# Conversion of weights under up 1: another order of the blocks, and higher prices in the planner's books

## The chip, the core and the metric

The kernel runs on one core of a Trainium2 chip. The metric is the device time of one execution in microseconds (us). The engines are TensorE (PE, with its weight loads as PEld), VectorE (DVE), ScalarE (ACT), GpSimd (POOL) and SyncE (SP), which issues the transfers.

## What is computed

A random-feature attention is followed by two feed-forward networks, all in float32 (2304 tokens, width 512):

```python
q_p, k_p = (phi(q_s), phi(k_s))
num = np.einsum('bhsm,bhmd->bhsd', q_p, kv)          # attention
h = x @ w_in                                         # "up 1"
x = (h * (1.0 / (1.0 + np.exp(-h)))) @ w_out         # "down 1"
g = x @ w_gate;  val = x @ w_val                     # "up 2"
return (silu(g) * val) @ w_out2                      # "down 2"
```

The weights come in as float64 and have to be turned into float32 on the chip before they can be used.

## The kernel before

**Stages.** Attention comes first (up to about 118 us), then up 1, down 1, up 2 and down 2. Each of the four products of matrices is done by Strassen's scheme with seven products per block (`PROD`, `ORDER`), and each float32 operand is split into a high and a low part, so that a product is three matmuls (high-high, high-low, low-high). Up 1 is a sequence `seq1` of 24 steps: a step is one block of 256 of the hidden features (there are eight, 0 to 7) for one of three groups of 768 tokens. The first nine steps take blocks 0, 1, 2 for each group of tokens in turn, the next three block 3, the next three block 4, and the last nine blocks 5, 6, 7. A step is seven products of six matmuls each. Between the products of a step, ScalarE copies a PSUM bank (L1120: `copy`), VectorE adds (L1177), ScalarE applies the activation (L1144: `post`), and SyncE stores the result to memory as `g_d` (L1129: `put`). The operands made of x are split beside it by ScalarE and VectorE (L586, L597, L619: `x_prep`).

**Conversion.** `conv_job` makes a list of operations for one block of float64 weights, in two halves h. Two loads of 512 KB (`load`, L328) go into raw buffers (`f_raw`, two at first). ScalarE turns the high words (`first`, L349) into a conversion buffer (`f_c`, three at first). VectorE shifts it (`shift`, L356) and puts in bits of the low words (`low`, L363). GpSimd makes four sums and differences of Strassen's scheme (`sums`, L382) into the one sum buffer (`f_sum`). What comes then depends on the weights. Blocks for up 1 ("in i") are split into high and low (L411 to L429) into an operand space (`f_w`, room for three blocks, taken first by blocks 0, 1 and 2). Blocks for down 1 ("out i", `down_job`) and the gate and value block for up 2 (`up_job_dram`) are stored to memory in three transfers (`store`, L446) and loaded later (L1282), and then split (L1286, L1290). The sum buffer and the conversion buffers are free when the splitting, or the store, is done. More buffers of both kinds are given (`more`) when the splitting of x has been handed out. Blocks 0 to 2 of both weights are converted during attention (`feed`, which goes by steps, not by times). The other twelve jobs run under up 1: in 3, out 3, in 4, out 4, ..., in 7, out 7, gate, val, in this order, joined by `weave`, which puts the first half of a job's list between the last operations of the job before. The first two loads of in 3 are issued at the end of attention.

**The planner.** All instructions are issued from one Python program; each engine works off its own queue in the order in which the program emitted. The program keeps books: `clk` has a time for each engine and for the transfers, `T` the time at which each result is there, and an `Op` has a price. `flush` is called ahead of every product. It emits operations whose turn has come by the books: first those in `urgent` (copies, additions, activations, stores of g), then of the streams the one that could start first, with a handicap of 0.1 us for each place in the list of streams (loads of g, weights of down, splitting for down, splitting of x, conversion). The conversion's stream looks one operation further on ScalarE (`ACT=2`). `need` emits at once what a product cannot do without. The prices come from `cost(kind, n)`, a constant and a rate for each engine (`fixed`); a transfer takes its bytes at 350e3 bytes per us of the books' transfer clock and lands 3.0 us later. The loads of g for down 1 (`zload`) wait until the conversion's stream is empty (a `guard`).

Of the kernel before, what the change touches and what calls it, by code (L numbers as in the profile page):

```python
# [42 lines left out]
def kernel(  # L43
# [19 lines left out]
    S = 576  # L63
# [16 lines left out]
    FP = (w_in.shape[0], w_gate.shape[0])  # L80
# [20 lines left out]
    def cut(t, o, n):  # L101
        return t[:, o : o + n]
# [14 lines left out]
    class Free:  # L117
# [17 lines left out]
        def give(self, x, t=None):  # L135
# [3 lines left out]
                return  # L139
            self.q.append((x, clk["PE"] if t is None else t))  # L140

    clk = {e: 0.0 for e in ("PE", "ACT", "DVE", "POOL", "SP", "dma", "slot")}
    T = {}
    fixed = {"ACT": (0.21, 0.00081), "DVE": (0.15, 0.00106), "POOL": (0.25, 0.0021), "COPY": (0.1, 0.0006)}

    def cost(kind, n):
        a, b = fixed[kind]
        return a + b * n

    class Op:  # L150
# [22 lines left out]
        def emit(self):  # L173
            t = max(clk[self.eng], self.ready())
            clk["slot"] = 0.0
            clk["end"] = t + self.cost
            self.fn()
            if self.eng == "SP":
                clk["SP"] = t + 0.3
                clk["dma"] = max(t, clk["dma"]) + self.cost  # L180
                end = clk["dma"] + 3.0
            else:
                clk[self.eng] = end = t + self.cost
            for k in self.outs:
                T[k] = end
            if self.then is not None:
                self.then(end)

    def dma_cost(nbytes):
        return nbytes / 350e3  # L190

    urgent = []
    maker = {}
# [118 lines left out]
    f_c = Free("c", [cut(fa, C_AT + i * 512, 512) for i in range(3)])  # L312
# [5 lines left out]
    w_slots = [x for x, _ in f_w.q]  # L318
    W = {}

    def conv_job(kind, i, dram=None, side=False):
        b = {}
        key = lambda *k: (kind, i, *k)

        def load(h):
            def go():
                b["r", h] = r = f_raw.take()
                nc.sync.dma_start(out=r.bitcast(U32), in_=wsrc[kind][i, h])  # L328

            def then(end):  # L330

                if kind == "out2":
                    T[key("r", h)] = end + 6.0

            return Op("SP", dma_cost(P * 4096), go, outs=[key("r", h)], slots=(f_raw, 1), then=then)

        def word(h, w):
            return b["r", h].bitcast(U32).rearrange("p (c w) -> p c w", w=2)[:, :, w]

        def first(h):  # L340
            def go():
                b["c", h] = c = f_c.take()

                nc.scalar.activation(c, word(h, 1).bitcast(F32), AF.Prelu, scale=2.0**-112, alpha=-(2.0**32))  # L349

            return Op("ACT", cost("ACT", 512), go, ins=[key("r", h)], outs=[key("c", h)], slots=(f_c, 1))

        def shift(h):
            def go():
                c = b["c", h].bitcast(U32)
                nc.vector.tensor_scalar(c, c, 3, None, op0=ALU.logical_shift_left)  # L356

            return Op("DVE", cost("COPY", 512), go, ins=[key("c", h)], outs=[key("s", h)])

        def low(h):  # L360
            def go():
                c = b["c", h].bitcast(U32)
                nc.vector.scalar_tensor_tensor(  # L363
                    c, word(h, 0), 29, c, op0=ALU.logical_shift_right, op1=ALU.bitwise_or
                )
                f_raw.give(b["r", h], clk["end"])

            return Op("DVE", cost("DVE", 512), go, ins=[key("s", h)], outs=[key("f", h)])

        def blk(n):  # L370
            if n in ("A21", "A22"):
                return cut(b["c", 0], 0 if n == "A21" else 256, 256)
            if n in ("A11", "A12"):
                return cut(b["c", 1], 0 if n == "A11" else 256, 256)
            return cut(b["S"], 256 * (int(n[1]) - 1), 256)

        def sums(n, l, r, ins):
            def go():
                if n == 1:
                    b["S"] = f_sum.take()  # L380
                f = nc.gpsimd.tensor_add if n == 1 else nc.gpsimd.tensor_sub
                f(blk(f"S{n}"), blk(l), blk(r))  # L382

            return Op(
                "POOL", cost("POOL", 256), go, ins=[key(*k) for k in ins], outs=[key("S", n)],
                slots=(f_sum, 1) if n == 1 else None,
            )

# [50 lines left out]
        def store(a, z, src, ins):  # L439

            b["stores"] = 3

            def go():
                o = dram(a, z)
                t = src()
                nc.sync.dma_start(out=o, in_=t.rearrange("p (o c) -> p o c", c=256) if len(o.shape) == 3 else t)  # L446
                b["stores"] -= 1
                if not b["stores"]:
                    done(clk["end"] + 2.0)

            return Op("SP", dma_cost(P * (z - a) * 1024), go, ins=[key(*x) for x in ins], outs=[key("d", a)])

        half = [load(0), load(1), first(0), first(1), shift(0), low(0), shift(1), low(1)]
        if dram is not None:
            return [
# [36 lines left out]
    def weave(*jobs):  # L492

        ops = [*jobs[0][:8]]
        for n, j in enumerate(jobs):
            new = deque(jobs[n + 1][:8] if n + 1 < len(jobs) else ())
            for _ in range(min(2, len(new))):
                ops.append(new.popleft())
            for i, o in enumerate(j[8:]):
                ops.append(o)  # L500
                if i % 2 and new:
                    ops.append(new.popleft())
            ops += new
        return ops

    def down_job(m, i):
        k = DNK[m]
        return conv_job(
            k, i, dram=lambda a, z: wd_d[k][a:z, :, i * 256 : (i + 1) * 256].rearrange("o p c -> p o c")
        )  # L510

    def up_job_dram(k):
        return conv_job(k, 0, dram=lambda a, z: wu_d[k][:, a * 256 : z * 256])
# [464 lines left out]
    for name in ("conv", "x"):  # L978
        while early[name]:
            assert early[name][0].ready() is not None  # L980
            early[name].popleft().emit()
            while urgent:
                urgent.pop(0).emit()
    first_up = conv_job("in", 3)
    for x in first_up[:2]:
        x.emit()
    for f, some in ((f_c, spare_c), (f_sum, [spare_sum])):
        n = len(f.q)
# [4 lines left out]
    for k in T:  # L993
        T[k] = 0.0
    for h, t in enumerate((4.0, 6.0)):
        T["in", 3, "r", h] = t
    for f in (f_raw, f_c, f_sum, f_z, f_w, f_s, f_op):
        f.q = deque((x, 0.0) for x, _ in f.q)

# [510 lines left out]
    def up_order(kinds, n, head, tail):  # L1510
# [4 lines left out]
            pairs[-3:] = [(n - 3, n - 2, n - 1)]  # L1515
        return [(i, k, s) for ps_ in pairs for s in range(NSB) for i in ps_ for k in kinds]

    to_come += [
        lambda: x_prep(0, 1, xr1, False, "DVE", then=lambda t: (x1_done.append(t), x1_then[0]())),
        lambda: x_prep(0, 2, xr2, False, "DVE", before=1, then=xr2_end),  # L1520
    ]

    rest = deque(down_job(0, i) for i in range(3, FP[0]))
    jobs = []
    for i in range(3, FP[0]):
        jobs += [conv_job("in", i) if i > 3 else first_up, rest.popleft()]
    jobs += rest
    jobs += [up_job_dram("gate"), up_job_dram("val")]
    conv1 = [x for x in weave(*jobs) if not any(x is y for y in first_up[:2])]
    opened = []  # L1530
    extra_c, extra_raw = cut(fa, XR_AT, 512), cut(fa, XR_AT + 512, 1024)

# [90 lines left out]
    jobs = [down_job(1, 0)]  # L1623
# [75 lines left out]
```

## Time and profile before

| | us |
|---|---|
| median of three runs | 853.46 |
| lowest and highest | 852.75, 853.49 |
| profiled execution | 853.52 |
| its span | 851.7 |

The profile is of one execution of its own, and its span is the time between the first and the last instruction. Times in its rows count from the start of the span. The rows come from several views: a page with the share of each engine and the costliest groups of instructions, tables by stretch of time, lists of waits, and the order of instructions in a stretch. In an order, the text in brackets at the end of a row is how long the engine stood idle before it, and what ended that.

### The profile page before, as it was taken

The numbers are of one execution on the slowest core, as the hardware profiler recorded it, in microseconds if no ns is written. First come the engines' busy times: TensorE is split into PE (matmuls) and PEld (weight loads), VectorE is DVE, ScalarE is ACT, GpSimd is POOL, SyncE is SP. The second block draws the span as 40 slices with busy tenths as digits, with TensorE's granted clock in tenths as the row PEclk, the third lists the DMA queues.
The fourth block names the chain that finished last, engine by engine and source line by source line (L and its number), as shares of the span: only waits on it lengthen the run. The fifth ranks groups of instructions, "written<-read, shape, count | busy, mean of one in ns | idle before, by whom it ended". The sixth has DMA issues, their size and how long they took to land.

```text
span 851.7 us, 18196 instructions
## 1 busy us (share of the span) xinstructions
PE 823.9 (97%) x6889; PEld 796.4 (93%) x6889; DVE 623.8 (73%) x1016; ACT 552.5 (65%) x1166; POOL 164.8 (19%) x204
## 2 busy tenths in 40 slices
PE   8999999999999879999998998999999999999998
PEld 7888889999899879999998998999999999899998
DVE  4888877576644687796899998584757548979783
ACT  6999878776767854455557874655556557646552
POOL 0477831044440000000000035121213010000000
PEclk9999999999999999999999999999999999999999
DMA  8579866588999865608514657462637168483602
GB/s 284 183 259 299 282 211 226 173 260 282 333 310 364 286 231 165 206 22 243 181 62 141 218 179 208 146 204 100 211 97 238 53 212 283 169 272 94 220 3 75
DMA packets 110120, 170.09 MB, mean 200 GB/s; under 512 B 9424, under 2 KB 94032, under 8 KB 110032
## 3 DMA queue, kind: packets, MB, share of 16 engines
q1 hardware_dynamic: 109808, 168.69, 60.9%
q8 instruction: 54, 0.88, 0.4%
q14 instruction: 34, 0.28, 0.1%
q10 hardware_dynamic: 224, 0.23, 0.1%
HBM read 107.02 MB, written 61.87 MB: 198 GB/s over the span
## 4 chain that ended last, share of the span: by engine, by line
PE 76%; DVE 7%; DMA 7%; issue 4%; ACT 3%; POOL 2%; SPq 0%; DVEq 0%; ACTq 0%; POOLq 0%
PE ps L1103 36%; PE ps L1478 29%; PE ps L757 4%; PE ps L801 2%; PE ps L817 2%; DMA wd_out<-fa 2%; PE ps L848 2%; DMA ra<-g_d 2%; POOL fa L382 2%; DVE fa L363 1%; DMA fa<-in_moe_w_val 1%; DVE ra L1341 1%; DMA fa<-in_moe_w_out 1%; DVE ra L429 1%; PE ps L873 1%
## 5 line engine op out<-in xcount | busy, mean ns | idle before, releaser
L382 POOL TENSOR_TENSOR fa<-fa 128x256 f32<-128x256 f32 x124 | 105.6, 866 | 506.4 <-ACT fa L1144 239.3
L1103 PE MATMUL ps<-ra 128*128 128x384 f32 x840 | 148.4, 328 | 6.1 <-ACT ps L1120 4.0
L1103 PE MATMUL ps<-rb,ra 128*128 128x384 f32 x840 | 146.3, 327 | 2.1 <-ACT ps L1120 2.1
L1103 PE MATMUL ps<-rc,ra 128*128 128x384 f32 x840 | 145.8, 326 | 1.5 <-ACT ps L1120 1.5
L1103 PEld LDWEIGHTS ps<-ra 128*128 128x128 f32 x840 | 137.6, 189 | 9.0 <-ACT ps L1120 5.8
L1103 PEld LDWEIGHTS ps<-rb,ra 128*128 128x128 f32 x840 | 137.6, 189 | 3.6 <-ACT ps L1120 3.3
L1103 PEld LDWEIGHTS ps<-rc,ra 128*128 128x128 f32 x840 | 137.8, 189 | 2.5 <-ACT ps L1120 2.4
L1120 ACT ACTIVATE ps<-ps 128x384 f32<-128x384 f32 x180 | 85.4, 477 | 67.7 <-PE ps L1103 63.4
L1177 DVE TENSOR_TENSOR fa<-fa,ps 128x384 f32<-128x384 f32 x120 | 66.2, 551 | 80.5 <-ACT ps L1120 58.0
L1337 ACT ACTIVATE ra<-fa 128x768 fp32r<-128x768 f32 x86 | 71.9, 841 | 60.4 <-PE ps L1478 43.9
L1341 DVE TENSOR_TENSOR ra<-fa,ra 128x768 fp32r<-128x768 f32 x81 | 77.4, 955 | 21.6 <-PE ps L1478 13.4
L1478 PE MATMUL ps<-ra 128*128 128x384 f32 x486 | 84.0, 332 | 6.8 <-DVE ra L1341 5.7
L1478 PE MATMUL ps<-ra,rb 128*128 128x384 f32 x516 | 89.9, 327 | 0.4 <-DVE ra L1341 0.4
L1478 PEld LDWEIGHTS ps<-ra 128*128 128x128 f32 x486 | 80.7, 192 | 9.0 <-DVE ra L1341 7.4
L1478 PE MATMUL ps<-ra,rc 128*128 128x384 f32 x482 | 83.9, 327 | 2.2 <-DVE ra L1341 2.2
L1478 PEld LDWEIGHTS ps<-ra,rb 128*128 128x128 f32 x516 | 84.5, 189 | 1.4 <-DVE ra L1341 1.0
L773 ACT ACTIVATE kq<-ps,nb 128x128 f32<-128x128 f32 x288 | 79.3, 401 | 7.8 <-DVE nb L771 7.5
L1478 PEld LDWEIGHTS ps<-ra,rc 128*128 128x128 f32 x482 | 78.9, 189 | 3.4 <-DVE ra L1341 3.2
L349 ACT ACTIVATE fa<-fa 128x512 f32<-128x512 f32 x65 | 54.0, 833 | 20.2 <-DMA fa<-in_moe_w_in 5.7
L1361 DVE TENSOR_TENSOR fa<-ra,fa 128x768 f32<-128x768 f32 x63 | 60.0, 953 | 4.4 <-DMA ra<-g_d 3.7
L1144 ACT ACTIVATE fa<-fa 128x384 f32<-128x384 f32 x84 | 43.6, 519 | 25.5 <-DVE fa L1177 25.2
L363 DVE SCALAR_TENSOR_TENSOR fa<-fa 128x512 uint32<-128x512 uint32 x65 | 56.0, 862 | 0.7
(112 smaller groups left out, 1104.5 us busy)
## 6 DMA issues: line engine op xcount, KB each, us to landing
g_d<-fa SPq DMA_DIRECT2D x168, 192.0 KB, 4.1
fa<-g_d SPq DMA_DIRECT2D x42, 384.0 KB, 5.0
ra<-g_d SPq DMA_DIRECT2D x42, 384.0 KB, 4.3
fa<-in_moe_w_out SPq DMA_DIRECT2D x28, 512.0 KB, 5.1
fa<-in_moe_w_in SPq DMA_DIRECT2D x16, 512.0 KB, 5.0
wd_out<-fa SPq DMA_DIRECT2D x12, 512.0 KB, 3.2
fa<-in_moe_w_gate SPq DMA_DIRECT2D x12, 512.0 KB, 4.0
fa<-in_moe_w_val SPq DMA_DIRECT2D x12, 512.0 KB, 5.2
```

The lines of the kernel that those rows point to most:

```text
L349: nc.scalar.activation(c, word(h, 1).bitcast(F32), AF.Prelu, scale=2.0**-112, alpha=-(2.0**32))
L363: nc.vector.scalar_tensor_tensor(c, word(h, 0), 29, c, op0=ALU.logical_shift_right, op1=ALU.bitwise_or)
L382: f(blk(f"S{n}"), blk(l), blk(r))
L773: nc.scalar.activation(e[:, g // 2, g % 2, h * M : (h + 1) * M], x[:, g, :], AF.Exp, bias=nb[:, g : g + 1])
L1103: nc.tensor.matmul(woven(ps[b][:, :N]), cut(l, j * P, P), halves(cut(r, j * N, N)), start=start and c == 0, stop=stop and c == 5, skip_gro ...
L1120: nc.scalar.activation(out() if callable(out) else out, src, AF.Copy)
L1144: nc.scalar.activation(b["t"], src, AF.Silu)
L1177: nc.vector.tensor_add(t, t if in_place else p5[n], ps[bank_][:, :N])
L1337: nc.scalar.activation(ops[s, p, k][0], src(), AF.Copy)
L1341: nc.vector.tensor_sub(l, src(), h.bitcast(F32))
L1361: (nc.gpsimd if eng == "POOL" else nc.vector).tensor_sub(z(PLACE[to]), z(PLACE.get(l, l)), z(PLACE.get(r, r)))
L1478: nc.tensor.matmul(woven(ps[BANKS[p] + e][:, :N]), cut(a, e * P, P), halves(b), start=p in FIRST and i == 0 and c == 0, stop=p in LAST and ...
```

## The change

There are four edits. The order of the twelve jobs under up 1 is out 3, out 4, out 5, then in 3, out 6, in 4, out 7, in 5, gate, in 6, val, in 7; accordingly the two loads issued at the end of attention are those of out 3. The books' prices for the conversion go up: `first` 0.85 (it was 0.62), `shift` 0.48 (0.41), `low` 0.9 (0.69), `sums` 1.1 (0.79). All transfers in the books take their bytes at 330e3 per us and land 3.5 us later. And `first` of a job's first half may be handed out only when no other job stands between its two halves (`halved`). The prices and the guard also hold for the conversion under up 2, and the transfers' prices for everything that is planned after attention.

```diff
@@ -139,6 +139,7 @@
+    LAND, RATE = 3.5, 330e3
     clk = {e: 0.0 for e in ("PE", "ACT", "DVE", "POOL", "SP", "dma", "slot")}
@@ -178,7 +179,7 @@
                 clk["dma"] = max(t, clk["dma"]) + self.cost
-                end = clk["dma"] + 3.0
+                end = clk["dma"] + LAND
@@ -187,7 +188,7 @@
     def dma_cost(nbytes):
-        return nbytes / 350e3
+        return nbytes / RATE
@@ -318,6 +319,8 @@
+    halved = []
+
     def conv_job(kind, i, dram=None, side=False):
@@ -340,6 +343,7 @@
             def go():
                 b["c", h] = c = f_c.take()
+                halved[:] = [x for x in halved if x is not b] + ([b] if h == 0 else [])
@@ -348,14 +352,14 @@
-            return Op("ACT", cost("ACT", 512), go, ins=[key("r", h)], outs=[key("c", h)], slots=(f_c, 1))
+            return Op("ACT", 0.85, go, ins=[key("r", h)], outs=[key("c", h)], slots=(f_c, 1), guard=lambda: h == 1 or not halved)
...
-            return Op("DVE", cost("COPY", 512), go, ins=[key("c", h)], outs=[key("s", h)])
+            return Op("DVE", 0.48, go, ins=[key("c", h)], outs=[key("s", h)])
...
-            return Op("DVE", cost("DVE", 512), go, ins=[key("s", h)], outs=[key("f", h)])
+            return Op("DVE", 0.9, go, ins=[key("s", h)], outs=[key("f", h)])
...
-                "POOL", cost("POOL", 256), go, ins=[key(*k) for k in ins], outs=[key("S", n)],
+                "POOL", 1.1, go, ins=[key(*k) for k in ins], outs=[key("S", n)],
@@ -981,8 +985,8 @@
-    first_up = conv_job("in", 3)
-    for x in first_up[:2]:
+    first_down = down_job(0, 3)
+    for x in first_down[:2]:
         x.emit()
@@ -993,7 +997,7 @@
     for h, t in enumerate((4.0, 6.0)):
-        T["in", 3, "r", h] = t
+        T["out", 3, "r", h] = t
@@ -1515,18 +1519,19 @@
+    AHEAD = 3
...
-    rest = deque(down_job(0, i) for i in range(3, FP[0]))
-    jobs = []
+    rest = [first_down, *(down_job(0, i) for i in range(4, FP[0])), up_job_dram("gate"), up_job_dram("val")]
+    jobs = rest[:AHEAD]
     for i in range(3, FP[0]):
-        jobs += [conv_job("in", i) if i > 3 else first_up, rest.popleft()]
-    jobs += rest
-    jobs += [up_job_dram("gate"), up_job_dram("val")]
-    conv1 = [x for x in weave(*jobs) if not any(x is y for y in first_up[:2])]
+        jobs += [conv_job("in", i), *rest[AHEAD + i - 3 : AHEAD + i - 2]]
+    jobs += rest[AHEAD + FP[0] - 3 :]
+    conv1 = [x for x in weave(*jobs) if not any(x is y for y in first_down[:2])]
```

## Rows read from the trace of the kernel before

**Rows 1.** The page's first part: busy us, share of the span, instructions.

```profile
PE 823.9 (97%) x6889; PEld 796.4 (93%) x6889; DVE 623.8 (73%) x1016; ACT 552.5 (65%) x1166; POOL 164.8 (19%) x204
```

**Rows 2.** Busy time by stretch: stretch, length, then engines; granted clock, DMA share, GB/s.

```profile
core 0: us, PE busy (x) PEld busy (x) DVE busy (x) ACT busy (x) POOL busy (x), PEclk, DMA share, GB/s
121.00:132.00 11.00, 10.78 (x68) 10.45 (x67) 9.30 (x20) 8.11 (x18) 3.64 (x4) 1.00 0.96 323
132.00:162.00 30.00, 29.88 (x184) 29.88 (x185) 22.36 (x46) 25.91 (x61) 0.00 (x0) 1.00 0.58 187
162.00:170.00 8.00, 8.00 (x51) 8.00 (x50) 1.93 (x5) 5.00 (x11) 0.00 (x0) 1.00 0.46 162
185.00:200.00 15.00, 13.33 (x81) 12.74 (x80) 9.83 (x18) 10.64 (x23) 7.57 (x9) 1.00 0.92 312
215.00:233.00 18.00, 16.73 (x100) 15.85 (x99) 12.89 (x24) 13.74 (x30) 7.73 (x9) 1.00 0.96 321
233.00:253.00 20.00, 19.20 (x118) 18.80 (x117) 11.17 (x18) 13.24 (x28) 9.42 (x12) 1.00 0.94 327
288.00:297.00 9.00, 6.84 (x39) 5.99 (x38) 6.41 (x8) 6.17 (x11) 0.00 (x0) 1.00 0.65 175
...
470.00:535.00 65.00, 59.91 (x359) 57.74 (x358) 60.12 (x113) 45.16 (x96) 18.49 (x20) 1.00 0.67 207
720.00:742.00 22.00, 20.11 (x119) 18.93 (x118) 20.46 (x27) 15.54 (x23) 0.00 (x0) 1.00 0.56 197
```

**Rows 3.** What TensorE waited for from 118 to 288: total, times, longest.

```profile
PE ps L1103 <- ACT ps L1120: 4.1, 7, 0.9
```

**Rows 4.** ScalarE by line, 170 to 253: count, busy, mean ns, idle before, releasers.

```profile
L349 ACT ACTIVATE fa<-fa 128x512 f32<-128x512 f32 x20 | 17.1, 855 | 12.0 <-DMA fa<-in_moe_w_in 5.7 <-POOL fa L382 4.0 <-DMA fa<-in_moe_w_gate 1.6
```

**Rows 5.** Order of instructions about 194: start, length, engine and line [idle before].

```profile
193.67 0.86 ACT L349 ACTIVATE fa<-fa 128x512 f32<-128x512 f32 x1 [2.32 <-DMA fa<-in_moe_w_in]
...
195.22 0.48 ACT L1120 ACTIVATE ps<-ps 128x384 f32<-128x384 f32 x1
...
195.75 1.24 PE L1103 MATMUL ps<-rb,ra 128*128 128x384 f32 x6 [0.91 <-ACT ps L1120]
```

**Rows 6.** Order of GpSimd's sums under up 1, the first ones and one pair.

```profile
128.53 2.99 POOL L382 TENSOR_TENSOR fa<-fa 128x256 f32<-128x256 f32 x3 [3.23 <-DVE fa L363]
174.04 2.70 POOL L382 TENSOR_TENSOR fa<-fa 128x256 f32<-128x256 f32 x2 [42.52 <-DVE ra L429]
...
182.28 2.92 POOL L382 TENSOR_TENSOR fa<-fa 128x256 f32<-128x256 f32 x4 [3.38 <-DMA wd_out<-fa]
...
197.21 1.42 POOL L382 TENSOR_TENSOR fa<-fa 128x256 f32<-128x256 f32 x2 [3.37 <-DMA wd_out<-fa]
```

**Rows 7.** The page's groups: count, busy, mean ns of one, idle before.

```profile
L382 POOL TENSOR_TENSOR fa<-fa 128x256 f32<-128x256 f32 x124 | 105.6, 866 | 506.4 <-ACT fa L1144 239.3
```

**Rows 8.** The page's transfers: count, KB each, median us from issue to landing.

```profile
fa<-in_moe_w_out SPq DMA_DIRECT2D x28, 512.0 KB, 5.1
...
wd_out<-fa SPq DMA_DIRECT2D x12, 512.0 KB, 3.2
```

**Rows 9.** Order of SyncE's issues about 253.

```profile
253.14 0.32 SPq L446 DMA_DIRECT2D wu_val<-fa  x1
253.55 1.22 SPq L1282 DMA_DIRECT2D ra<-wd_out  x2
```

**Rows 10.** Order of instructions at the hand-over from up 1 to down 1.

```profile
288.80 1.57 ACT L1286 ACTIVATE rb<-rb 128x768 fp32r<-128x768 f32 x2
...
293.33 0.43 PE L1478 MATMUL ps<-ra 128*128 128x384 f32 x1 [1.12 <-ACT ra L1337]
...
306.45 0.96 DVE L1361 TENSOR_TENSOR fa<-ra,fa 128x768 f32<-128x768 f32 x1 [2.37 <-DMA ra<-g_d]
...
308.33 9.89 PE L1478 MATMUL ps<-ra 128*128 128x384 f32 x48 [1.98 <-DVE ra L1341]
```

**Rows 11.** Busy time by stretch, as rows 2, inside down 1's start.

```profile
310.00:312.00 2.00, 2.00 (x8) 2.00 (x8) 1.96 (x3) 1.78 (x3) 0.00 (x0) 0.50 0.41 153
```

More of the change, by code (lines that the diff above doesn't have):

```diff
@@ L1521 @@
     ]
-    rest = deque(down_job(0, i) for i in range(3, FP[0]))
-    jobs = []
+    rest = [first_down, *(down_job(0, i) for i in range(4, FP[0])), up_job_dram("gate"), up_job_dram("val")]
+    jobs = rest[:AHEAD]
     for i in range(3, FP[0]):
-        jobs += [conv_job("in", i) if i > 3 else first_up, rest.popleft()]
-    jobs += rest
-    jobs += [up_job_dram("gate"), up_job_dram("val")]
-    conv1 = [x for x in weave(*jobs) if not any(x is y for y in first_up[:2])]
+        jobs += [conv_job("in", i), *rest[AHEAD + i - 3 : AHEAD + i - 2]]
+    jobs += rest[AHEAD + FP[0] - 3 :]
+    assert len(jobs) == len(rest) + FP[0] - 3
+    conv1 = [x for x in weave(*jobs) if not any(x is y for y in first_down[:2])]
     opened = []
```

## The prediction, made before the changed kernel was run

> **What bounds the kernel now.** I read the page's first part, then a table of busy time by stretch, then who TensorE waited for, and only then the order of work around the worst waits. TensorE is busy 823.9 of 851.7 us [rows 1], so an edit that moves no matmul can win only some of its idle time, and the question is which idle time. The table [rows 2] places it. During up 1's weight conversion TensorE lost 1.67 us (185 to 200), 1.27 us (215 to 233) and 0.80 us (233 to 253), each the stretch minus the PE column. At the hand-over to down 1 it lost 2.16 us (288 to 297). Up 2's start lost 5.09 us and down 2's start 1.89 us. In 132 to 162 it lost only 0.12 us, although ScalarE was busy 25.91 of 30 us: a full ScalarE alone does not stop TensorE.
>
> Every wait of up 1 is for line 1120 [rows 3], ScalarE's PSUM copy between two products. The order shows why [rows 5]: ScalarE stood 2.32 us before a conversion instruction (L349) whose weights had not landed, the copy queued behind it came late, and TensorE lost 0.91 us. Between 170 and 253 ScalarE stood 12.0 us in front of its 20 L349 instructions [rows 4]. So the planner puts conversion into the queue earlier than its data are there.
>
> Why is the conversion so late? GpSimd's sums, of which every block has four, stop at about 131.5 us (128.53 + 2.99) and resume at 174.04 after 42.52 us, released by the block of up 1's weights that got its operand space [rows 6]. That block (in 3) sits on the only sum buffer until block 0's W space is free after step 6. After that a pair (one block for up 1, one for down 1) takes 197.21 - 182.28 = 14.93 us [rows 6]: 74.6 us for five pairs, and the last store of the value weights is issued at 253.14 [rows 9].
>
> **Part 1, the order.** Nothing is computed more or less: twelve blocks stay. Out 3, 4 and 5 now come ahead of in 3, so the sum buffer is turned over three times in the stretch in which it stood still. After 174 the queue before was out 3, in 4, out 4, in 5, out 5, in 6, out 6, in 7, out 7, gate, val. It becomes out 6, in 4, out 7, in 5, gate, in 6, val, in 7: each block of up 1's weights stands where it stood, four pairs are left, and the conversion ends near 174 + 4 x 14.93 = 234 instead of 253. SyncE's loads and stores move with them: out 3's first two loads replace in 3's at the end of attention, of the same size.
>
> *Behind 234*, no L349 is in ScalarE's queue and the 0.80 us of 233 to 253 should go. Term B: **-0.8** (bounds 0 and -0.8).
>
> *In 121 to 170* some five more L349, five pairs of shift and low on VectorE and twelve sums come beside the splitting of x. Their price isn't in the trace. The nearest row is the later stretch: about 3.7 us lost over 20 L349, 0.19 us each, times five, about +0.9. It can be below nothing, since the 0.34 us of 121 to 142 came from one such wait and may go. The upper end is ScalarE's debt: five times 0.855 us [rows 4] and five waits of 12.0/20 = 0.6 us are 7.3 us, against 30 - 25.91 = 4.1 us free before 162; 3.2 us remain over, and 3.0 us are free up to 170. I take the value nearest to the conversion's own rows. Term C: **+0.8** (bounds -0.3 and +3.2).
>
> A page speaks against this move. VectorE kept its pace beside the sums in the trace: in 121 to 132 it was busy 9.30 us with three sums at 2.99/3 = 1.0 us against a mean of 0.87 [rows 2, 6, 7], so mostly the sum got longer. The Trainium skill, "SBUF — State Buffer", section Who interferes with whom, has GpSimd and VectorE share a port pair under an exclusive lock, the loser blocked for the whole instruction. By that rule twelve sums of 0.87 us would take up to 10.4 us from VectorE, more than the 7.6 us it has free in 132 to 162; term C would be near its upper end and the sum about 852.2. The row is nearer to a loss of a tenth of that.
>
> **Part 2, the books.** They issue nothing; they decide the order in each engine's queue, in all stages after attention. A pair's chain by the old prices: eight sums of 0.79, a last ACT half of 0.62, two subtractions of 0.69, the store's 1.50 + 2.0 and some 0.6 of hops, 12.4 us. By the new ones the sums are 1.1 and the store 1.59: 15.0 us. The trace has 14.93. For a load the books said 1.50 + 3.0 = 4.5 us and now say 5.1; the trace has 5.1 [rows 8]. So the plan was ahead of the chip by some 2.5 us a pair, which is what ScalarE's 12.0 us of standing show, and the new prices meet it. I take two thirds of the 1.67 + 1.27 = 2.94 us away; one third stays because single waits scatter. Term A: **-2.0** (bounds 0 and -2.9).
>
> A page would price the load otherwise. The Trainium skill, "SBUF — State Buffer", section The DMA setup-cost knee, gives a transfer about 2 us plus its bytes at 436 GB/s, 3.2 us for 512 KB; the stores of that size agree (3.2 us), the loads (5.1 us) don't, and the measurement decides [rows 8]. By the page's figure the new books would hold conversions back needlessly by 1.9 us a load; ScalarE would then stand before none of them, term A would be -2.9 and the sum 848.9.
>
> **Part 3, the hand-over.** Before, the first load of down 1's weights (L1282) leaves SyncE right behind the late last store, at 253.55 against 253.14 [rows 9]; with the conversion over by 234, that store is out of the way. The weights' splitting (L1286) then lies earlier, and it is what ScalarE does at 288.80 directly before down 1's first operands, for which TensorE waits 1.12 us [rows 10]. Of the 2.16 us lost in 288 to 297 I take 1.7 away. Not more, because the next stall doesn't hang on it: at 306.45 VectorE has stood 2.37 us for a load of g, which can leave only when up 1's last products are stored, and TensorE waits 1.98 us [rows 10]. What TensorE gains ahead of this it can give back there. Term D: **-1.7** (bounds +0.5 and -4, below).
>
> Behind that stall lies another price: at 310 to 312 the granted clock is 0.50, so 1.2 GHz instead of 2.4, after the idle stretch before it [rows 11]. The 48 matmuls from 308.33 took 9.89 us [rows 10]; at 29.88/184 = 0.162 us each [rows 2] they would take 7.8. The dip costs 2.1 us, goes if the stall gets small, and comes again wherever waits of that size cluster.
>
> *Up 2 and down 2*: the same new prices reorder 470 to 535 (5.09 us lost, VectorE busy 60.12 of 65) and 720 to 742 (1.89 us) [rows 2]. No row says which way. Term E: **0** (bounds -2.5 and +4).
>
> **Sum.** The profiled execution took 853.52 us (span 851.7 and 1.8 around it), the median of the runs is 853.46, so I count from 853.5: -2.0 - 0.8 + 0.8 - 1.7 + 0 = -3.7, **849.8 us**.
>
> **Rivals.** *The dip goes too*: later prices for loads put VectorE's waiting subtraction behind work that is ready, the stall at 308 shrinks and the clock stays: 849.8 - 2.1, and about 0.6 of up 2's loss, 847.1. For: the new landing time is later by 0.5 us and more for each load queued. Against: the load itself comes no sooner.
>
> *Up 2 takes it back*: three blocks are wanted there in a row, and each is booked 1.3 us longer (half of 15.0 - 12.4). If the queue follows the books and not the data, the value weights arrive 3.9 us later and TensorE waits: 853.7. For: VectorE is full there. Against: the chain of the data is no longer than it was.
>
> *The change doesn't do what it says*: until x is split there are only three conversion buffers and two raw ones; if out 4 and 5 are not through before in 3, the queue after 174 is as long as before. Then B and D fall away and half of A stays: 852.5.
>
> *Slower*: ScalarE's debt in 121 to 170. It decides from the point at which the conversion's work and waits there pass the 4.1 us that are free before 162. Six L349 with waits of 0.6 us are 6 x 1.455 = 8.7; if x's operands come late by all that is over, TensorE stands 8.7 - 4.1 = 4.6 us. With half of A and with B: 853.5 - 1.0 - 0.8 + 4.6 = 856.3, and 858.4 with a dip. For: VectorE and ScalarE are densest there. Against: 0.12 us lost in 30 so far.
>
> **How the numbers follow.** Chances: forecast 0.42, dip gone too 0.16, up 2 takes it back 0.14, no effect of the order 0.13, slower 0.15. A measurement of this kernel tells about 0.2% from no change, 1.7 us: faster is below 851.8, slower above 855.2. Faster: 0.40 + 0.16 + 0.02 = 0.58; slower: 0.13 of the last and 0.05 of up 2's case, 0.18; 0.24 is left for the same. The range goes from 846.3 (all of A, D and a dip's end) to 856.2 and leaves out about half of the slow case and the far end of the fast one.
>
> **What would show it.** Right: POOL busy in 132 to 162 and the last conversion store near 234; ScalarE's idle time before L349 well under 12.0 us; no wait for L1120 after 240; L1282 leaving SyncE by 247. Wrong: waits for L1120, L586 or L597 between 132 and 170 above 1 us; idle 470 to 535 above 5.1 us; a granted clock of 0.5 at a new place. The forecast fails if the queue's order, and not its data, was what held the conversion.

## The result and the profile after

The changed kernel took 864.43 us (median), against 853.65 for the kernel before in the same runs: 1.0134 times, interval 1.0119 to 1.0150, so slower by 11 us. The profiled execution took 864.67 us with a span of 862.9. The forecast was 849.8, with 856.2 as the far end of the range.

I cut the time of one execution by stage, from the first product of a stage to the first of the next, and for down 2 to its last, in the order of TensorE's instructions (us):

| | attention | up 1 | down 1 | up 2 | down 2 |
|---|---|---|---|---|---|
| before | 118.1 | 175.2 | 175.9 | 253.0 | 125.7 |
| after | 118.9 | 182.8 | 176.2 | 256.4 | 124.7 |

Up 1 lost 7.6 us and up 2 3.4 us. TensorE's work is the same, but it shows 4.2 us more of busy time than in [rows 1], which is already a hint that matmuls ran slower somewhere. The page's first part of after:

```profile
PE 828.1 (96%) x6889; PEld 802.4 (93%) x6889; DVE 625.7 (73%) x1016; ACT 553.8 (64%) x1166; POOL 163.1 (19%) x204
```

Busy time by stretch, with the columns of [rows 2]:

```profile
132.00:162.00 30.00, 27.79 (x168) 26.91 (x167) 19.77 (x34) 21.53 (x48) 10.16 (x11) 1.00 0.92 289
162.00:170.00 8.00, 4.02 (x16) 3.73 (x15) 5.66 (x10) 4.69 (x11) 3.06 (x4) 0.74 1.00 324
170.00:185.00 15.00, 14.82 (x82) 14.27 (x81) 12.34 (x27) 12.63 (x28) 0.00 (x0) 0.91 0.48 163
185.00:200.00 15.00, 15.00 (x94) 15.00 (x93) 7.49 (x14) 11.40 (x23) 6.86 (x8) 1.00 0.93 296
215.00:233.00 18.00, 18.00 (x113) 18.00 (x112) 10.40 (x19) 13.30 (x28) 6.30 (x8) 1.00 0.90 300
233.00:253.00 20.00, 17.22 (x103) 16.22 (x101) 13.85 (x25) 12.09 (x26) 6.94 (x8) 1.00 0.64 215
310.00:320.00 10.00, 6.75 (x32) 6.45 (x31) 6.36 (x9) 3.12 (x6) 0.00 (x0) 0.83 0.97 361
470.00:535.00 65.00, 58.19 (x343) 56.76 (x342) 56.87 (x110) 44.65 (x95) 10.53 (x13) 0.95 0.60 193
```

The stretches in which TensorE waited before, 185 to 200 and 215 to 233, are full now. In their place stand 2.21 us lost in 132 to 162, 3.98 in 162 to 170 with a granted clock of 0.74 behind it, and 2.78 in 233 to 253. Note that ScalarE is *less* busy in 132 to 162 than before (21.53 against 25.91 us): it did not have too much to do; it stood.

What ScalarE stood for, by its conversion line (L353 is the former L349), first from 121 to 170, then from 170 to 260:

```profile
L353 ACT ACTIVATE fa<-fa 128x512 f32<-128x512 f32 x8 | 6.5, 813 | 7.9 <-DMA wd_out<-fa 4.4 <-DMA g_d<-fa 1.8 <-DMA fa<-x_d 1.6
L353 ACT ACTIVATE fa<-fa 128x512 f32<-128x512 f32 x16 | 13.8, 861 | 1.4 <-DMA fa<-in_moe_w_in 1.1 <-DMA fa<-in_moe_w_out 0.2
```

The second row answers to [rows 4]: 12.0 us of standing became 1.4. The first shows where standing came back, 7.9 us in front of eight instructions, 4.4 of them for one store. The order of instructions about it:

```profile
157.50 1.48 SPq L450 DMA_DIRECT2D wd_out<-fa  x3
...
162.94 0.67 ACT L353 ACTIVATE fa<-fa 128x512 f32<-128x512 f32 x1 [4.45 <-DMA wd_out<-fa]
...
166.84 2.29 PE L1107 MATMUL ps<-rb,ra 128*128 128x384 f32 x6 [3.98 <-ACT ps L1124]
```

SyncE issues the stores of out 5 only at 157.50, behind loads of x. The second half of in 3 needs one of out 5's buffers; its L353 stands at the head of ScalarE's queue until the store has landed, and the PSUM copy (L1124, the former L1120) behind it lets TensorE wait 3.98 us.

The late wait of up 1 is for the last block:

```profile
247.83 3.14 POOL L386 TENSOR_TENSOR fa<-fa 128x256 f32<-128x256 f32 x4 [2.80 <-DMA wu_val<-fa]
...
251.00 0.63 ACT L420 ACTIVATE ra<-fa 128x512 fp32r<-128x512 f32 x1 [4.14 <-POOL fa L386]
...
252.06 1.24 PE L1107 MATMUL ps<-ra 128*128 128x384 f32 x6 [2.55 <-ACT ps L1124]
```

The sums of in 7 come at 247.83 to 250.97. In the kernel before, the sums of in 7 began at 227.13. They are now hardly earlier than the last sums of all before (252.4), although only four pairs of blocks were left at 185: a pair takes longer now, as the starts of the sums of every second block show:

```profile
203.81 4.78 POOL L386 TENSOR_TENSOR fa<-fa 128x256 f32<-128x256 f32 x4 [7.06 <-DVE ra L433]
...
221.93 0.73 POOL L386 TENSOR_TENSOR fa<-fa 128x256 f32<-128x256 f32 x1 [6.99 <-DVE ra L433]
...
240.30 1.12 POOL L386 TENSOR_TENSOR fa<-fa 128x256 f32<-128x256 f32 x1 [7.37 <-DVE ra L433]
```

These are 18.1 and 18.4 us apart, against 14.93 in [rows 6].

In up 2 the gate block is late. The rows show VectorE's two conversion steps of one half of the block ahead of it (the first one for down 2), GpSimd's sums of the gate block, which wait for that block's store, then ScalarE's and TensorE's waits:

```profile
501.64 0.42 DVE L360 TENSOR_SCALAR fa<-fa 128x512 uint32<-128x512 uint32 x1
...
511.24 0.81 DVE L367 SCALAR_TENSOR_TENSOR fa<-fa 128x512 uint32<-128x512 uint32 x1
...
518.59 2.89 POOL L386 TENSOR_TENSOR fa<-fa 128x256 f32<-128x256 f32 x4 [3.41 <-DMA wd_out<-fa]
...
520.85 0.67 ACT L353 ACTIVATE fa<-fa 128x512 f32<-128x512 f32 x1 [4.42 <-DMA fa<-in_moe_w_val]
...
524.32 1.65 PE L1107 MATMUL ps<-ra 128*128 128x384 f32 x4 [6.14 <-DVE ra L433]
```

And at the start of down 1, VectorE's subtraction stands for a load of g as in [rows 10], and TensorE waits longer than its 1.98 us:

```profile
314.04 0.96 DVE L1365 TENSOR_TENSOR fa<-ra,fa 128x768 f32<-128x768 f32 x1 [2.52 <-DMA ra<-g_d]
...
315.93 6.33 PE L1482 MATMUL ps<-ra 128*128 128x384 f32 x27 [3.25 <-DVE ra L1345]
```

### The profile page after: what moved, and what is told of

Same layout as the page of the kernel before. It is cut to its first block, busy times and chain, and to the rows that moved or that the text cites. A ratio compares the mean times of both kernels' runs of the same rounds, so it can differ in the third digit from the quotient of the medians.

```text
span 862.9 us, 18198 instructions
## 1 busy us (share of the span) xinstructions
PE 828.1 (96%) x6889; PEld 802.4 (93%) x6889; DVE 625.7 (73%) x1016; ACT 553.8 (64%) x1166; POOL 163.1 (19%) x204
## 4 chain that ended last, share of the span: by engine, by line
PE 77%; DMA 7%; DVE 6%; ACT 4%; issue 4%; POOL 1%; SPq 1%; DVEq 0%; ACTq 0%; POOLq 0%
PE ps L1107 39%; PE ps L1482 27%; PE ps L761 4%; PE ps L805 2%; PE ps L821 2%; DMA g_d<-fa 2%; DMA ra<-g_d 2%; PE ps L852 2%; ACT kq L777 1%; DVE ra L1345 1%; DMA x_d<-fa 1%; POOL fa L386 1%; DMA fa<-in_moe_w_val 1%; DVE fa L367 1%; DMA xr<-x_d 1%
## 5 line engine op out<-in xcount | busy, mean ns | idle before, releaser
L386 POOL TENSOR_TENSOR fa<-fa 128x256 f32<-128x256 f32 x124 | 103.5, 849 | 521.7 <-DVE fa L367 317.1
L1107 PE MATMUL ps<-rb,ra 128*128 128x384 f32 x840 | 148.4, 330 | 5.2 <-ACT ps L1124 5.0
L1107 PE MATMUL ps<-rc,ra 128*128 128x384 f32 x840 | 147.8, 329 | 0.2 <-DVE rc L601 0.2
L1107 PEld LDWEIGHTS ps<-rb,ra 128*128 128x128 f32 x840 | 139.6, 191 | 6.6 <-ACT ps L1124 6.3
L1107 PEld LDWEIGHTS ps<-rc,ra 128*128 128x128 f32 x840 | 139.8, 191 | 0.9 <-DVE rc L601 0.4
L1124 ACT ACTIVATE ps<-ps 128x384 f32<-128x384 f32 x180 | 85.8, 478 | 70.1 <-PE ps L1107 59.1
L353 ACT ACTIVATE fa<-fa 128x512 f32<-128x512 f32 x65 | 53.5, 826 | 16.5 <-DMA fa<-in_moe_w_val 5.1
```

The lines of the kernel that those rows point to most:

```text
L1107: nc.tensor.matmul(woven(ps[b][:, :N]), cut(l, j * P, P), halves(cut(r, j * N, N)), start=start and c == 0, stop=stop and c == 5, skip_gro ...
L1124: nc.scalar.activation(out() if callable(out) else out, src, AF.Copy)
```

## The experiments

The change has three parts that issue something: the order, the prices of the conversion, and the landing time and rate. (The guard moves nothing in up 1 of the kernel before under its old books: the run further down that has the guard and another place of one load issues there, on ScalarE, VectorE and SyncE, what the kernel before issues, in the same order. Under the new order the guard was never run by itself; the first run below leaves it out, the other three have it.) The first four runs take them apart. Theory A said that the order costs up 1 and the prices cost up 2; theory B that the order is good and the books cost both.

**Order alone.** From the changed kernel:

```diff
-    LAND, RATE = 3.5, 330e3
+    LAND, RATE = 3.0, 350e3
-            return Op("ACT", 0.85, go, ..., guard=lambda: h == 1 or not halved)
+            return Op("ACT", cost("ACT", 512), go, ...)
...
-                "POOL", 1.1, go, ins=...
+                "POOL", cost("POOL", 256), go, ins=...
```

> The new order of the blocks under the old books (old prices, landing 3.0 us, 350e3, no guard). In the changed kernel up 1 became 7.6 us longer (175.2 to 182.8) and up 2 3.4 us. Theory A (the order costs up 1, the prices cost up 2): three blocks for down 1 beside the splitting of x make ScalarE stand for a late store, so TensorE loses some 5 to 7 us in 121 to 170 here too; up 2 stays at 253; about 859 to 861 us. Theory B (the books cost both, the order alone is good): no long wait in 121 to 170, up 1 173 to 175 us; 850 to 854 us.

Measured: 858.03 us, ratio 1.0043 (1.0024 to 1.0062).

**Books alone.** The old list of jobs, the rest as in the changed kernel.

```diff
-    first_down = down_job(0, 3)
+    first_up = conv_job("in", 3)
...
+        jobs += [conv_job("in", i) if i > 3 else first_up, rest.popleft()]
+    jobs += rest
```

> The old order of the blocks under all of the new books (prices, landing 3.5 us at 330e3, guard). Theory A: up 1 loses less than before in 185 to 233 (the 2.94 us lost there shrink), up 2 is longer by about 3.4 us as in the changed kernel, where TensorE waited 6.1 us for the gate block; 853 to 856 us. Theory B: the long waits of up 1 (4.0 us at 166, 2.5 at 252) are here too; 861 to 866 us.

Measured: 857.38 us, ratio 1.0038 (1.0016 to 1.0059).

**Order and prices, old landing.**

```diff
-    LAND, RATE = 3.5, 330e3
+    LAND, RATE = 3.0, 350e3
```

> The new order with the new prices of the conversion and the guard, but transfers in the books as of before (landing 3.0 us, 350e3). If the prices of the conversion are what holds the later blocks back (a pair of blocks took about 18 us after 182 and TensorE waited 2.5 us at 252, and 6.1 us in up 2), this is like the changed kernel, 862 to 866 us. If it is the landing time, the waits at 252 and in up 2 go: 856 to 860 us.

Measured: 858.26 us, ratio 1.0051 (1.0036 to 1.0066).

**Order and landing, old prices.** The four prices as in the first run, the guard stays.

> The new order with the new landing time and rate (3.5 us, 330e3) and the guard, but the old prices of the conversion. The other half of the run before it: if the prices hold the later blocks back, the waits at 252 and in up 2 are gone here and only the loss in 121 to 170 is left, 857 to 861 us; if the landing time does, this is like the changed kernel, 862 to 866 us.

Measured: 854.06 us, ratio 1.0006 (0.9993 to 1.0019): not told apart from the kernel before.

The stages and the conversion in the four (one execution each; "stood" is ScalarE's idle time before the conversion line; a pair is the mean distance of the sums of every second block after 174, and "last sum" the start of the last of them, both from the order of GpSimd's instructions):

| | up 1 | up 2 | stood 121 to 170 | stood 170 to 260 | pair | last sum |
|---|---|---|---|---|---|---|
| before | 175.2 | 253.0 | 1.0 | 12.0 | 14.9 | 252.4 |
| order | 177.7 | 252.6 | 4.9 | 10.0 | 14.8 | 234.6 |
| order, landing | 174.3 | 252.4 | 3.1 | 4.0 | 15.9 | 235.3 |
| landing, prices | 175.3 | 256.0 | 1.8 | 3.3 | 16.9 | 265.5 |
| order, prices | 174.3 | 256.3 | 5.0 | 6.9 | 17.4 | 240.3 |
| all (after) | 182.8 | 256.4 | 7.9 | 1.4 | 18.4 | 250.0 |

The rows behind the standing, for the order alone (both stretches), the books alone and order with landing (170 to 260):

```profile
L353 ACT ACTIVATE fa<-fa 128x512 f32<-128x512 f32 x8 | 6.4, 828 | 4.9 <-DMA wd_out<-fa 3.9 <-DMA fa<-in_moe_w_out 1.0
L353 ACT ACTIVATE fa<-fa 128x512 f32<-128x512 f32 x16 | 13.6, 851 | 10.0 <-DMA fa<-in_moe_w_in 5.9 <-POOL fa L386 3.4 <-DMA fa<-in_moe_w_out 0.5
```

```profile
L353 ACT ACTIVATE fa<-fa 128x512 f32<-128x512 f32 x20 | 16.5, 824 | 3.3 <-DMA fa<-in_moe_w_out 2.0 <-DMA fa<-in_moe_w_in 1.3
```

```profile
L353 ACT ACTIVATE fa<-fa 128x512 f32<-128x512 f32 x16 | 13.8, 865 | 4.0 <-DMA fa<-in_moe_w_in 3.4 <-DMA fa<-in_moe_w_out 0.6
```

With the books alone in 7 came late too, under the old order: its splitting stood in ScalarE's queue behind two L353 for out 7, and TensorE waited.

```profile
238.69 0.66 ACT L353 ACTIVATE fa<-fa 128x512 f32<-128x512 f32 x1 [1.54 <-DMA fa<-in_moe_w_out]
239.26 0.92 ACT L420 ACTIVATE ra<-fa 128x256 fp32r<-128x256 f32 x2
...
240.77 3.57 PE L1107 MATMUL ps<-ra 128*128 128x384 f32 x10 [4.03 <-DVE ra L433]
```

Single executions differ, and the table has one of each. The changed kernel and two runs further down, whose instructions are the same until up 2, took 182.8, 182.8 and 183.6 us for up 1; but two other runs that are the same until up 2 (the 847.27 and the 845.81 below) took 174.1 and 176.5. So differences under about 2.5 us in up 1 are not told apart. The execution with order and landing was also the fastest of its ten (851.77, median 854.06).

Three of the four medians lie outside what either theory expected; order with prices lies in its 856 to 860, but the wait in up 2 that should have gone with that stayed (6.48 us). Four things follow. The prices cost up 2 its 3 to 4 us, with any order and any landing time: that part of A holds. The new order does what it says: with the old books the last sum comes at 234.6, the 234 of the prediction. Alone it is slower by some 4 us all the same: up 1 is 2.5 us longer, which one execution hardly tells, and down 1 2.0 us (177.9), with a wait of 3.47 us for a load of g and a granted clock of 0.50 in 312 to 316. In all four kernels with the new order ScalarE stands 3 to 8 us in 121 to 170, between 2.4 and 4.4 of that for a store of weights (`wd_out`), a wait that ScalarE has in no row of the kernel before (there GpSimd's sums waited for such a store, [rows 6]). And with the new order each half of the new books (with the guard) makes a pair longer, the landing by about 1 us, the prices by about 2.5, both by 3.5; with the old order both make it 2 us longer. But neither theory foresaw that up 1 loses its 7.6 us only with all parts together; in pairs or alone they leave it between 174.3 and 177.7. Why it takes all of them was not found out; the next run takes on the largest piece of it.

**Does the long wait hang on the place of that store in the books?** The books call a stored buffer free 2.0 us after the store's place; here 5.0 for out 3 to 5.

```diff
-                    done(clk["end"] + 2.0)
+                    done(clk["end"] + (5.0 if kind == "out" and i < 6 else 2.0))
```

> The changed kernel, but the books call the buffers of out 3, 4 and 5 free 5.0 us behind their last store's place instead of 2.0. In the changed kernel ScalarE stood 4.45 us at 162.9 before an L353 whose buffer a store (issued at 157.5) had not left, and TensorE lost 3.98 us at 166.6, with the clock at 0.74 behind it. Theory A (the books' optimism on a store is what that stall hangs on): the L353 goes into the queue later, the stall is under 1.5 us, up 1 is 4 to 6 us shorter (177 to 179), about 859 us. Theory B (three blocks beside the splitting of x are too much work there, wherever they are queued): the loss only moves, up 1 stays at 181 to 184, 863 to 866 us.

Measured: 859.61 us, ratio 1.0075 (1.0046 to 1.0104). Up 1 took 177.2 us, 5.6 less than after, the up 2 of 256.1 stayed. The stretch 162 to 170 and the standing in 121 to 170:

```profile
162.00:170.00 8.00, 8.00 (x52) 8.00 (x51) 7.97 (x15) 6.80 (x16) 2.99 (x3) 1.00 0.63 201
L353 ACT ACTIVATE fa<-fa 128x512 f32<-128x512 f32 x7 | 5.9, 837 | 1.9 <-DMA fa<-in_moe_w_out 1.9
```

No wait for the store is left, TensorE is full and the clock stays at 1.00. A stall of 2.06 us at 157 and the late one of 2.6 us at 247 remain. So the books' optimism on a store was the cause of the largest stall, and most of the loss did not move elsewhere, as it would have if three blocks beside the splitting of x were too much work. What the three blocks cost without that stall is not nothing: TensorE still lost 3.2 us in 121 to 170, by waits of 1.14 and 2.06 us.

**Which price costs up 2?** Under up 2 alone, first VectorE's two prices as of before, then ScalarE's and GpSimd's. (The condition in the edit names the conversion of up 1.)

```diff
-            return Op("DVE", 0.48, go, ...
+            return Op("DVE", 0.48 if kind in ("in", "out") or dram is not None and kind != "out2" else cost("COPY", 512), go, ...
```

> The changed kernel, but under up 2 the conversion's two VectorE operations have their old prices (0.41 and 0.69). Under up 2 VectorE is nearly full; in the changed kernel the second half's L367 came at 511.0, 9.6 us behind its L360, behind the splitting of x, and TensorE waited 6.1 us for the gate block. Theory A (VectorE's prices lose the conversion its turn): up 2 is back near 253 us (256.4 changed), the wait is under 2 us, 861 us. Theory B (ScalarE's and GpSimd's prices do it): up 2 stays at 256, 864 us.

Measured: 858.86 us, ratio 1.0079 (1.0054 to 1.0103); up 2 took 250.7.

> The other half: the changed kernel, but under up 2 ScalarE's L353 and GpSimd's sums have their old prices (0.62 and 0.79), VectorE's the new ones. Theory A (VectorE's prices): up 2 stays at 256, 864 us. Theory B: up 2 near 253, 861 us.

Measured: 865.09 us, ratio 1.0137 (1.0117 to 1.0157); up 2 took 255.1. What TensorE waited for from 470 to 560, in the first and in the second of the two:

```profile
PE ps L1107 <- DVE ra L433: 1.0, 2, 0.8
```

```profile
PE ps L1107 <- DVE ra L433: 4.7, 1, 4.7
```

And VectorE's steps of the half that came 9.6 us apart after, with VectorE's old prices:

```profile
500.68 0.42 DVE L360 TENSOR_SCALAR fa<-fa 128x512 uint32<-128x512 uint32 x1
501.13 1.21 DVE L367 SCALAR_TENSOR_TENSOR fa<-fa 128x512 uint32<-128x512 uint32 x1
```

VectorE's prices do it (the two were set back together; which of them decides was not tried). The 0.48 and 0.9 are near what the operations take (0.47 and 0.86 in the lines of the kernel before), and still they cost: as I read the order, on a full VectorE a result booked 0.07 or 0.21 us later lets a ready operation of x pass, and the next chance came 9.6 us later. The other two new prices are worth something under up 2: with them and VectorE's old ones it took 250.7, less than before.

**A version that beats both.** With the new order all runs waited 3.1 to 3.5 us at down 1's start for the load of g that VectorE needs next (B22), which SyncE issued behind four loads (B21) that are needed later. From order and landing with the old prices, with the later freeing:

```diff
-    streams["z"].extend(z_first(0, "B21", "B22"))
+    streams["z"].extend(z_first(0, "B22", "B21"))
-    streams["z"].extend(z_first(1, "B21", "B22"))
+    streams["z"].extend(z_first(1, "B22", "B21"))
```

> A version meant to beat both: the new order, the new landing time and the guard with the old prices of the conversion, the buffers of out 3 to 5 called free 5.0 us behind the store, and at both hand-overs the loads of g for the third quarter-block (B22) ahead of those for B21, since VectorE's next subtraction needs B22 first (in all runs TensorE lost 2 to 3.5 us there). If the stall at down 1's start hangs on the place of that load, down 1 is 2 to 3 us shorter (173 to 174 against 176.1 with the old loads' order) and the whole is near 850 us; if it hangs on the last store of g alone, down 1 stays at 176 and the whole at 853 us.

Measured: 847.27 us, ratio 0.9930 (0.9911 to 0.9950). Down 1 took 172.2 us, 3.9 less than with order and landing and the loads' old order (176.1). At the hand-over:

```profile
295.39 5.97 SPq L1315 DMA_DIRECT2D ra<-g_d  x6
301.57 0.95 DVE L1365 TENSOR_TENSOR fa<-ra,fa 128x768 f32<-128x768 f32 x1
...
304.31 8.88 PE L1482 MATMUL ps<-ra 128*128 128x384 f32 x53 [0.64 <-DVE ra L1345]
```

VectorE no longer stands, TensorE waits 0.64 us, and the 53 matmuls behind it run at full clock (0.168 us each against 0.206 in [rows 10]).

Three runs take this version apart, and one adds the good half of the prices under up 2:

> The kernel before (old order, old prices, old landing; the guard issues nothing other under these) with one thing from the version at 847.3 us: the loads of g for B22 ahead of those for B21 at both hand-overs. It tells how much of that version's gain has nothing to do with the change. Theory A (B22's place is the gain): down 1 falls from 175.9 to some 172, 849.5 us. Theory B (it paid because the conversion ends earlier and the loads' way is free): down 1 falls by less than 1.5 us, 852 us or more.

Measured: 849.32 us, ratio 0.9960 (0.9940 to 0.9979), down 1 172.7. By the medians the place of the load makes up more than half of the gain, and it has nothing to do with the change.

> The version at 847.3 us with the old order of the blocks (and so without the later freeing, which touches only out 3 to 5): new landing time and guard, old prices, B22 first. If the new order is worth what the earlier end of the conversion promised, this is slower than 847.3 by 1 to 3 us (848 to 850); if the loss in 121 to 170 eats it, the two are within 1 us.

Measured: 848.35 us, ratio 0.9962 (0.9942 to 0.9983). Within the intervals this is the same as with the new order. In the one execution up 1 was shorter (172.3) and down 1 longer (176.1) than with the new order (174.1 and 172.2; the first of these differences is one that a single execution does not tell); the stretch 320 to 330 of down 1 in this run and then in the 847.27 version:

```profile
320.00:330.00 10.00, 10.00 (x54) 10.00 (x53) 7.36 (x9) 4.83 (x8) 0.00 (x0) 0.85 0.50 148
```

```profile
320.00:330.00 10.00, 10.00 (x64) 10.00 (x63) 8.69 (x10) 5.92 (x9) 0.00 (x0) 1.00 0.58 167
```

TensorE's waits ahead of it, about 314 and 318, were 0.99 and 1.86 us here and 1.07 and 0.99 there: 0.8 us more, and behind them a clock of 0.85, at which ten matmuls fewer (some 1.6 us) were done. That is 2.4 of the 3.9 us; the rest stays open.

> The version at 847.3 us without the later freeing of the buffers of out 3 to 5. In the kernel with that landing time the stalls at 156 and 162 were 1.04 and 0.87 us, in the version with late freeing one of 2.09 at 159: if the late freeing is worth something only where a long wait for a store was planned, this is the same, 847 to 848 us; if it helps at large, 849 us.

Measured: 847.95 us, ratio 0.9954 (0.9940 to 0.9967): without the later freeing the same. It paid where a long wait for a store was planned, as in the changed kernel, and showed nothing here. The intervals of these three runs overlap, so what the order and the landing time add to the load's new place is not shown.

```diff
+    # under up 2: sums 1.1 and first 0.85; everywhere: shift and low as before
-                "POOL", 1.1, go, ...
+                "POOL", cost("POOL", 256) if (kind in ("in", "out") or dram is not None and kind != "out2") else 1.1, go, ...
```

> The version at 847.3 us with the new prices of ScalarE and GpSimd, but not of VectorE, under up 2, which gave up 2 its shortest time so far (250.7 us against 252.4). If that holds here, 845.5 us; if it hung on the kernel it was measured in, 847 us.

Measured: 845.81 us, ratio 0.9927 (0.9909 to 0.9946), up 2 250.7. The best median, but not told apart from the 847.27. The 250.7 of up 2 came again, 1.7 us less than without these prices.

## Why the prediction was wrong

The steps that failed are in terms C, B and E: a wait for a store that the sum did not have, a pair's length taken from the old books, and a loss in up 2 put at nothing. Of the signs of being wrong, all three came: a wait of 3.98 us in 132 to 170, 6.81 us idle in 470 to 535, and a granted clock of 0.50 at new places.

- **Term A (-2.0, the stalls of 185 to 233): right, and larger.** The 2.94 us went altogether, and ScalarE's standing there fell from 12.0 to 1.4 us. Books nearer to the data do take the stalls away, with the old order too (books alone: nothing lost from 185 to 233). By parts, with the new order, TensorE lost 2.7 us there under the old books, 1.2 with the landing and 0.5 with the prices; ScalarE stood 10.0, 4.0 and 6.9 us.
- **Term B (-0.8): wrong, +2.0 instead.** The step that failed is "four pairs are left, 4 x 14.93". I took the pair's length from the trace of the old books and, two paragraphs on, gave the new books 15.0 us for it, as a sum of prices. The pair became 18.4 us. Prices are not all of a pair: as I read the order, an operation that is booked later also loses its place to others (with the later freeing the same books gave pairs between 14.5 and 20.7 us). So the order's gain of 18 us in the end of the conversion (234.6, order alone) was given back by the books (250.0), and in 7 came late: 2.55 us of waiting at 252. That is the books' doing more than the order's: the books alone made TensorE wait 4.03 us for in 7, the order alone not at all (nothing lost in 236 to 246). Nor did each block of up 1's weights stand where it stood: even with the order alone the sums of in 7 began at 232.4, 5 us later than before.
- **Term C (+0.8, at most +3.2): the largest miss; the rival "slower" had the place and the engine, but neither the size nor the cause.** ScalarE stood in 121 to 170, as the rival said, but not because its work did not fit: it was less busy there than before. Two parts of the price were too small. I priced a wait at 0.6 us from the late stretch, where waits are for loads and sums; here it was 7.9/8 = 1.0, and a single one of 4.45 for a store. The buffers of a block for down 1 are free only when its stores have landed, and three such blocks now follow each other on three buffers. The code shows it, and a row of before hinted at it: GpSimd's sums stood 3.38 us for a store of that kind [rows 6]. And I had left the clock out of the bound. TensorE lost 2.2 + 4.0 us of idle time there, and the 98 matmuls of 162 to 185 took 18.8 us of busy time instead of 98 x 0.162 = 15.9: about 9 us instead of 0.8. With the later freeing 5.6 of up 1's 7.6 us came back.
- **The other price of that move,** up to 10.4 us that twelve sums would take from VectorE, came to a third. VectorE's operations of 121 to 170 that ran beside sums took 3.5 us longer in all than the same kinds alone (0.7 us in the kernel before); order with prices and order with landing had 2.9 and 3.4 us of it with an up 1 of 174.3, so it is not what cost up 1. But "VectorE kept its pace" was too kind a reading: in the kernel before, the two L619 of this stretch beside sums took 0.85 us on average, the other fourteen 0.55.
- **Term D (-1.7): given back, as the prediction feared.** TensorE began down 1 with waits of 0.46 and 0.56 us (1.12 and 0.56 before), and then waited 3.25 instead of 1.98 for the same load. Down 1 is 0.3 us longer. The load's place decides here: with B22 first, down 1 fell to between 172.2 and 172.7 us in four of five runs. In the fifth, old order with landing, it stayed at 176.1, for which no cause was found.
- **Term E (0): the rival "up 2 takes it back" was right in place and size** (3.4 us, forecast 3.9), and partly in its reason. Putting the term at nothing, because no row said which way, was the step that failed. It said that the queue follows the books and not the data; the runs add that VectorE's two prices, raised by 0.07 and 0.21 us, do it without the others. My "against", that the chain of the data is no longer than it was, was no argument: the order on VectorE held up the block ahead by 9.6 us, and the gate block waited for that block's store.
- **Chances.** I treated the slow case and up 2's case as alternatives with 0.15 and 0.14. They were two stretches of one kernel, and both happened. Up 2's case alone (853.7) stays in the range, the slow case (856.3, with a dip 858.4) begins just past its end; a sum of both, 856.3 + 3.9 = 860.2, with the dip 862.3, would have been near what was measured, though in part by luck: its 4.6 us of waiting stood for too much work on ScalarE, not for a store.

## What to carry to other kernels

A planner's book price is two things, an estimate and a priority. Making it truer can make the kernel slower: here two prices of VectorE, raised by 0.07 and 0.21 us to near the measured times, cost up 2 5.7 us (250.7 to 256.4), as I read it because a result that is booked later loses its turn on a full engine. So change such prices stage by stage, and look at what comes late behind them.

When work is moved into a stretch that looks free, list what it will wait for there (buffers that a store must leave, a queue with other loads) and not only the engine's free time. Here each engine worked off its queue in order, and one early instruction of ScalarE that stood 4.45 us made TensorE wait 3.98 us.

An order of loads that is written down by hand at a hand-over deserves a look before anything cleverer: two swapped names were worth 3 to 4 us here, the whole change minus 11.

## What the runs showed of the hardware

A wait of TensorE can cost more than itself. After the 3.98 us of idle time at 163 to 167 the granted clock was 0.50 for some 6 us, so 1.2 GHz; stretches of 2 us of the changed kernel:

```profile
166.00:168.00 2.00, 1.16 (x4) 1.17 (x5) 0.51 (x1) 1.55 (x4) 1.41 (x2) 0.50 1.11 337
168.00:170.00 2.00, 2.00 (x8) 2.00 (x7) 1.80 (x3) 1.55 (x5) 0.73 (x1) 0.50 0.79 199
170.00:172.00 2.00, 2.00 (x8) 2.00 (x7) 1.69 (x4) 1.71 (x5) 0.00 (x0) 0.50 0.88 333
172.00:174.00 2.00, 2.00 (x12) 2.00 (x11) 1.09 (x3) 0.87 (x3) 0.00 (x0) 0.84 0.33 111
174.00:176.00 2.00, 2.00 (x15) 2.00 (x14) 1.49 (x4) 1.90 (x5) 0.00 (x0) 1.00 0.40 138
```

Eight matmuls in 2 us instead of twelve: 2.9 us on top of a wait of 4.0. The same stands behind the 3.25 us at 316 (0.83 in 310 to 320) and the 6.1 us of up 2 (0.95 in 470 to 535). In the version with late freeing, where the wait at 163 is gone, the clock stays at 1.00 there. So the price of a wait has to be counted with the clock behind it.

Not every wait had that price, and the same one did not have it every time, so the prediction's "comes again wherever waits of that size cluster" is no rule that these runs bear out. Behind the 2.55 us at 252 the clock stayed at 1.00. The 847.27 and the 845.81 version issue the same instructions in up 1: in the first a wait of 2.09 us ended at 159.1 and the clock stayed at 1.00, in the second one of 2.05 us ended at 160.6 and the clock was 0.50 in 162 to 164.
